# Turning the decayed keys by DMA instead of on TensorE, in a fused linear-attention and feed-forward kernel

## The chip, the cores and the metric

The kernel runs on one core of one Trainium2 chip. The metric is the device time of one execution in microseconds, the median over runs. The core has a matrix engine (TensorE, PE in the profile; its weight loads have a row of their own, PEld), a vector engine (VectorE, DVE), a scalar engine (ScalarE, ACT), GpSimd (POOL), and a queue engine (SyncE, SP) that issues nearly all DMAs here. Each engine works through its own list of instructions in order and waits on semaphores for the others.

## The reference

Two parts, cut to what matters. The first is a linear attention with a decaying state (batch 4, 8 heads, 768 tokens, head size 48):

```python
state = zeros((B, H, D, D))
for t in range(S):
    cur = einsum('bhd,bhe->bhde', u[None] * kt, vt)
    y[:, :, t] = einsum('bhd,bhde->bhe', rt, state + cur)
    state = wt[:, :, :, None] * state + einsum('bhd,bhe->bhde', kt, vt)
```

The second takes the result as 3072 tokens of 384 and is a feed-forward block with 2048 hidden units:

```python
h = x @ w_in
g = h - tanh(h)
out = g @ w_out
```

All inputs and outputs are fp32, and the kernel works in fp32.

## The kernel before

**Blocks.** The 768 tokens of each of 4 sequences are cut in two, which gives eight blocks of 384 tokens (NB). A block has four pairs of heads (one pair fills the 128 partitions: two heads of 48 rows, padded to 64) and six chunks of 64 tokens. Heads are handled in two halves of two pairs each, named by their first pair: half 2 and half 0, in that order (HALVES).

**The attention of a block.** With the transposed keys, receptances and decays loaded with features on partitions, `behind` (L379) makes by a scan the product of the decays from each token to the end of its chunk, and `before` (L372) the same towards the chunk's beginning. `times_behind` (L397) multiplies the keys by the first; the result, the decayed keys, lies in the tile `post`. `earlier` (L462) multiplies decayed keys with decayed receptances within a chunk. `update_1` (L480) needs the decayed keys a second time, with tokens on partitions: `turn` (L465) transposes them on TensorE, twelve squares of 128x128 for a block (two halves, two pairs, three pairs of chunks), into a scratch tile of PSUM for each half, and ScalarE copies each half to the tile `ks` (L473). `update_2` (L500) forms the states, and the result of a block is gathered into `xT` by `result`, `result_out` (ScalarE copies) and `fill_holes` (six small DMAs, L618). `bound` (L414) is a check of the decays on ScalarE: one pass over a half of the tile `w`, with a sum.

**The feed-forward part.** For a block it runs over 16 slices of the hidden units, f = 0 to 15. `first` (L717) makes the hidden values of a slice, hp, by six matmul instructions (L720), and ScalarE copies them out as h (L723). The tile hp has one buffer. `slight` (L729) then squares on ScalarE (L741, L742, L744), and VectorE makes g (L726). In blocks 2 to 7 the second product is done in a form with fewer multiplications (`Fewer`, L821): sums of slices of g on VectorE (L767), products on TensorE (L835), and at a block's end scalings of the banks by ScalarE (`scaled`, L845) in f=1 and f=2 of the next pass. Block 0 and 1 use plain products (L797).

**The order of the work.** The order on TensorE, SyncE, VectorE and ScalarE is the order in which the program emits it. The loop over i (blocks) and f runs the feed-forward part of block i, and weaves in the attention of block i+1 (`later`) and the first scans of block i+2 (`after`). `plan` (L886) says at which f each piece is emitted: `phases` for TensorE's pieces, `before` and `ahead` for the others, `loads` for the DMAs. Within one f the order of emission is: h of this f and its squares; VectorE's waiting pieces; the entries of `before`; the phase; the entries of `ahead`; sums and loads; then second products that have come due and their scalings. In pass i=0 the plan is its own one; passes i=1 to 6 prepare blocks 2 to 7; i=7 prepares nothing. The first block's attention runs ahead of the loop (`boot`, L931) and uses `turn` as well, as does pass i=0 for block 1.

The tiles `w`, `k`, `r`, `post`, `pre` and `ks` have one buffer each, used by one block after the other.

Of the kernel before, what the change touches and what calls it, by code (L numbers as in the profile page):

```python
# [42 lines left out]
U16 = mybir.dt.uint16  # L43
# [8 lines left out]
P = 128  # L52
L = 64
NB = 384
# [6 lines left out]
HALF = WIDE // 2 + 2  # L61
UP = 2
# [58 lines left out]
def kernel(  # L121
# [12 lines left out]
    nc = tc.nc  # L134
# [146 lines left out]
    class Block:  # L281
# [183 lines left out]
        def turn(self, ps, p0, ahead=0):  # L465
# [6 lines left out]
                                        self.chunk("post", p0 + p, 2 * c, n=2), ident)  # L472
            nc.scalar.copy(out=ks.rearrange("t p c d -> t p (c d)"), in_=tp[:, :, 0:NCP * P])  # L473

        def keys(self):
            if not hasattr(self, "ks"):
                self.ks = work.tile([P, NPAIR, NCP, P], F32, name="ks", tag="ks", bufs=1)
            return self.ks
# [142 lines left out]
        def phase(self, ps, name):  # L621

            if name in ("own", "earlier"):
                return [getattr(self, name)(ps, p0) for p0 in HALVES]
            if name == "turn":
                for p0 in HALVES:
                    self.turn(ps, p0)
            elif name == "update":
                self.update_1(ps)
                return [self.update_2]  # L630
            elif name == "result 1":
                self.results(ps)
                self.result("from_states", ALL)
            elif name == "result 2":
                self.result("from_scores", ALL, True)
                self.result_out(ALL)
                self.fill_holes([nc.sync])
            return []
# [247 lines left out]
    def plan(i):  # L886


        converted = ()
        if i == 0:  # L890
            phases = {4: "turn", 6: "update", 8: "own", 11: "earlier", 13: "result 1"}
            before = {0: ("behind 2", "take_whole 2"), 1: ("behind 0", "take_whole 0", "times_behind 2"),
                      2: ("times_behind 0",), 3: ("before 2",), 4: ("times_u 2",), 5: ("before 0", "times_u 0"),
                      8: ("times_before", "held", "bound 2"), 9: ("bound 0",)}
            ahead = {}
            converted = range(READY + 1, NF)
            loads = {f: "weights" for f in (0, 1, 3, 4, 5, 6, 7, 8, 9, 10)}
            loads.update({2: "next r", 11: "w", 12: "k", 13: "r"})
        else:
            phases = {4: "earlier", 7: "turn", 10: "update", 12: "result 1"}  # L900
            before = {0: ("times_behind 2",), 1: ("times_behind 0",), 3: ("times_before", "held"), 4: ("bound 2",),
                      5: ("product_u",), 6: ("bound 0", "product_r"), 7: ("product_sum",), 8: ("diagonal_in 2",),
                      9: ("diagonal_in 0",)}
            if i == 1:
                phases = {6: "earlier", 8: "turn", 10: "update", 12: "result 1"}
                before.update({0: ("behind 2", "take_whole 2"), 1: ("behind 0", "take_whole 0"),
                               2: ("before 2", "times_behind 2"), 3: ("before 0", "times_behind 0"),
                               4: ("times_before", "held", "bound 2")})
            ahead = {10: ("behind 2", "take_whole 2"), 12: ("behind 0", "take_whole 0"), 13: ("before 2",),
                     15: ("before 0",)}  # L910
            loads = {1: "v", 3 + (i == 1): "tokens k", 4 + (i == 1): "tokens r", 7: "w", 9: "k", 11: "r"}
        return phases, before, ahead, converted, loads
# [113 lines left out]
    for i, blk in enumerate(blocks):  # L1026
# [5 lines left out]
        if i == 1:  # L1032
            early.close()
            if fast:
                wide = ctx.enter_context(tc.tile_pool(name="wide", bufs=1))
                forms = wide.tile([P, NF // 2, len(W_FORMS), P], F32, name="forms", tag="forms")
                G = wide.tile([P, 32, P], F32, name="g", tag="g")
        phases, before, ahead, converted, loads = plan(i)
        row0 = blk.b * S + blk.q * NB
        fewer = Fewer(row0, acc, few[i] // 2) if few[i] else None  # L1040
        second = Second(row0, acc, few[i]) if few[i] < NF else None
        for f in range(NF):
# [37 lines left out]
            if not later and f == NF - 2:  # L1080
                at = n_whole + n_excess
# [21 lines left out]
            name, ins = loads.get(f), None  # L1103
# [20 lines left out]
            while due and due[0][0] <= now:  # L1124
                _, add, what = due.pop(0)
# [84 lines left out]
```

## Time and profile before

| What | Value |
|---|---|
| time, three runs | 573.3, 573.57, 575.57 us (median 573.57) |
| span of the profiled execution, first to last instruction | 572.0 us (the page gives no time of its own for this execution) |
| TensorE busy | 553.3 us, 97% |
| VectorE busy | 477.7 us, 84% |
| ScalarE busy | 345.3 us, 60% |
| granted TensorE clock, mean | 0.999 |
| DMA | 50.40 MB, mean 88 GB/s |
| transposes on TensorE (L471) | 96, of which 72 in the passes i=1 to 6 |
| copies of them on ScalarE (L473) | 16, mean 789 ns |

The profile is of one execution. Busy time is a share of the span; durations of matmuls overlap, so the distance from one start to the next is what a matmul costs in a full stretch. A group's idle time is that of its engine just before it, with the releaser behind the arrow. In a timeline a row is: start, length (of the whole group, if several are merged), engine, line, operation, output and input, count, and in brackets the idle time before it. Pass i=4 begins its first products (f=0) at 300.93 us, and the f that follow begin at 306.22, 310.16, 313.44, 316.71, 321.74, 325.02, 328.29, 332.88, 336.15 and 342.11 us (f=1 to 10). The transposes of the passes i=1 to 6 begin at 134.54, 197.58, 264.04, 330.23, 396.41 and 462.72 us.

### The profile page before, as it was taken

How to read it: one execution, taken by the hardware profiler on the slowest of the kernel's cores; microseconds unless marked ns; L12 is line 12 of the kernel's file. 1: busy time of each engine (PE TensorE's matmuls, PEld its weight loads, DVE VectorE, ACT ScalarE, POOL GpSimd, SP SyncE). 2: the span in 40 equal slices, each digit the busy share in tenths (PEclk: the TensorE clock that was granted, in tenths of full speed). 3: DMA queues.
4: the chain of work that ended last, by engine and by line, in shares of the span. 5: the costliest groups of instructions: out<-in, count | busy, mean ns of one | idle time of the engine just before them, and what ended most of it. 6: DMA issues, size and time to landing. Idle time of an engine off the chain costs nothing.

```text
span 572.0 us, 14041 instructions
## 1 busy us (share of the span) xinstructions
PE 553.3 (97%) x5736; PEld 404.7 (71%) x5736; DVE 477.7 (84%) x926; ACT 345.3 (60%) x702; POOL 11.9 (2%) x40
## 2 busy tenths in 40 slices
PE   4889999999999999999999999999999999999996
PEld 4646666566665887777778787777878777787763
DVE  8878884799879989889998989989998998658673
ACT  3979893343137755577566775767556775667441
POOL 6100000000000000000000000000000000000000
PEclk9999999999999999999999999999999999999999
DMA  8496553222203232041212231122221300100101
GB/s 323 174 333 208 180 181 109 83 84 76 92 11 107 69 105 64 5 125 57 74 62 72 84 113 57 53 84 85 72 66 49 120 2 2 44 10 1 41 2 45
DMA packets 32453, 50.40 MB, mean 88 GB/s; under 512 B 2560, under 2 KB 30336, under 8 KB 32384
## 3 DMA queue, kind: packets, MB, share of 16 engines
q1 hardware_dynamic: 32144, 49.38, 26.9%
q8 instruction: 46, 0.75, 0.6%
q14 instruction: 23, 0.19, 0.1%
q0 software_dynamic: 96, 0.07, 0.1%
q10 hardware_dynamic: 144, 0.00, 0.0%
HBM read 43.55 MB, written 4.72 MB: 84 GB/s over the span
## 4 chain that ended last, share of the span: by engine, by line
PE 92%; ACT 2%; DVE 2%; DMA 2%; issue 1%; SPq 0%; DVEq 0%
PE hp L720 42%; PE acc L835 22%; PE acc L797 13%; PE att L835 5%; PE att L447 2%; PE att L471 2%; PE att L561 2%; PE att L496 2%; PE att L578 2%; ACT up L255 1%; DMA r<-in_rT 1%; DMA w<-in_wT 1%; DVE post L387 1%; DVE post L401 0%; ACT w_sb L255 0%
## 5 line engine op out<-in xcount | busy, mean ns | idle before, releaser
L720 PE MATMUL hp<-xT,w_sb 128*128 128x384 f32 x768 | 270.1, 488 | 2.0 <-ACT h L723 1.4
L720 PEld LDWEIGHTS hp<-xT,w_sb 128*128 128x128 f32 x768 | 138.4, 190 | 81.7 <-ACT h L723 4.4
L723 ACT ACTIVATE h<-hp 128x384 f32<-128x384 f32 x128 | 62.6, 489 | 150.2 <-PE hp L720 148.5
L835 PE MATMUL acc<-forms,g 128*128 128x128 f32 x810 | 121.1, 277 | 0.5
L835 PEld LDWEIGHTS acc<-forms,g 128*128 128x128 f32 x810 | 108.7, 192 | 15.6 <-issue 1.2
L767 DVE TENSOR_TENSOR g<-g 128x256 f32<-128x256 f32 x225 | 95.5, 424 | 19.8 <-DVE g L767 0.9
L726 DVE SCALAR_TENSOR_TENSOR h<-h,s 128x384 f32<-128x384 f32 x128 | 70.5, 550 | 10.6 <-ACT s L741 9.9
L797 PE MATMUL acc<-w_sb,sums 128*128 128x384 f32 x192 | 68.1, 491 | 1.6 <-DVE sums L726 1.3
L726 DVE SCALAR_TENSOR_TENSOR g<-qa,h 128x384 f32<-128x384 f32 x96 | 53.6, 558 | 17.1 <-PE acc L835 4.0
L742 ACT ACTIVATE qa<-s,shift 128x384 f32<-128x384 f32 x90 | 55.4, 615 | 2.9
L744 ACT ACTIVATE junk<-s,shift 128x384 bf16<-128x384 f32 x90 | 53.9, 599 | 0.0
L797 PEld LDWEIGHTS acc<-w_sb,sums 128*128 128x128 f32 x192 | 35.6, 190 | 25.9 <-DVE sums L726 2.6
L741 ACT ACTIVATE s<-h 128x384 f32<-128x384 f32 x90 | 47.1, 523 | 2.9
L835 PE MATMUL acc<-w_sb,g 128*128 128x128 f32 x270 | 44.9, 275 | 0.0
L752 ACT ACTIVATE qa<-s,shift 128x384 f32<-128x384 f32 x38 | 23.2, 611 | 24.7 <-DVE top L749 24.7
L835 PEld LDWEIGHTS acc<-w_sb,g 128*128 128x128 f32 x270 | 37.4, 192 | 0.0
L749 DVE CUSTOM_DVE_ANT_0 s<-h 128x384 f32<-128x384 f32 x38 | 21.0, 553 | 12.8 <-ACT h L723 12.8
L255 ACT ACTIVATE up<-raw 128x768 f16<-128x768 f32 (+1 forms) x32 | 31.7, 1056 | 0.0
L726 DVE SCALAR_TENSOR_TENSOR sums<-qa,h 128x384 f32<-128x384 f32 x32 | 17.9, 558 | 15.6 <-ACT qa L752 12.2
L835 PE MATMUL att<-w_sb,g 128*128 128x128 f32 x180 | 30.2, 275 | 0.0
L835 PEld LDWEIGHTS att<-w_sb,g 128*128 128x128 f32 x180 | 26.4, 192 | 4.5
L387 DVE TENSOR_TENSOR_SCAN post<-w,seed 128x780 f32<-128x780 f32 x16 | 28.5, 1784 | 1.1 <-DMA w<-in_wT 1.0
(87 smaller groups left out, 529.1 us busy)
## 6 DMA issues: line engine op xcount, KB each, us to landing
raw<-in_weights SPq DMA_DIRECT2D x16, 768.0 KB, 4.4
w<-in_wT SPq DMA_DIRECT2D x7, 780.0 KB, 4.6
k<-in_kT SPq DMA_DIRECT2D x7, 768.0 KB, 4.7
r<-in_rT SPq DMA_DIRECT2D x7, 768.0 KB, 4.5
v_sb<-in_v SPq DMA_DIRECT2D x8, 576.0 KB, 4.2
k<-in_tokens SPq DMA_DIRECT2D x6, 576.0 KB, 3.9
r<-in_tokens SPq DMA_DIRECT2D x6, 576.0 KB, 4.0
out_y<-sums SPq DMA_DIRECT2D x15, 128.0 KB, 1.9
```

The costliest lines, as they stand in the source:

```text
L255: return lambda: nc.scalar.activation(out=to, in_=of, func=AF.Copy, scale=scale, bias=bias)
L387: return nc.vector.tensor_tensor_scan(out=back(t[:, 0:width]), data0=back(self.tile("w")[:, a:a + width]), data1=back(seed[:, 0:width]), i ...
L720: nc.tensor.matmul(hp, lhsT=w_in_sb[:, f, kc, :], rhs=xT[kc], start=(kc == KC - 1), stop=(kc == 0))
L723: return h, nc.scalar.activation(out=h, in_=hp, func=AF.Copy, scale=1.0 / UPSCALE)
L726: return lambda: nc.vector.scalar_tensor_tensor(out=out, in0=in0, scalar=scalar, in1=in1, op0=op0, op1=ALU.mult)
L741: nc.scalar.activation(out=s, in_=h, func=AF.Square)
L742: nc.scalar.activation(out=qa, in_=s, func=AF.Square, bias=shift[:, 4:5])
L744: nc.scalar.activation(out=junk[:, 0:NB], in_=s, func=AF.Relu, bias=shift[:, 5:6], accum_out=excess[:, at:at + 1])
L752: first = [lambda: nc.scalar.activation(out=qa, in_=s, func=AF.Square, bias=shift[:, 4:5])]
L767: return lambda: nc.vector.tensor_tensor(out=G[:, to:to + 2], in0=two(G, g_at(q, a0), g_at(q, a1)), in1=two(G, g_at(q, b0), g_at(q, b1)), ...
L797: nc.tensor.matmul(acc, lhsT=g[:, j * P:(j + 1) * P], rhs=w_out_sb[:, f, :], start=(f == self.first), stop=(f == NF - 1))
L835: nc.tensor.matmul(to, lhsT=G[:, g_at(q, a), :], rhs=rhs, start=start, stop=stop, skip_group_check=True)
```

## The change

For the six blocks that are prepared in passes i=1 to 6 the phase "turn" is taken out of the plan. In its place stand four phases, two for each half:

- `split` copies a half of the decayed keys on ScalarE, read as 16-bit words, into two planes (all low halves of the 32-bit values, then all high halves). Then SyncE issues one DMA that transposes the planes in squares of 128x128 16-bit elements. Half 2 uses the second half of the tile `w` for its planes and the place of half 0 in `ks` for the result; half 0 uses the place of half 2 in `post` for the planes and its own place in `post` for the result.
- `join` copies the transposed planes on ScalarE back into 32-bit values in `ks`, as 16-bit words.

A half is 128 partitions of 768 fp32 values, 1536 words of 16 bits. In passes i=2 to 6 the phases stand at f=2 (split 2), f=5 (join 2), f=6 (split 0) and f=9 (join 0), and bound 2 moves from f=4 to f=1. In pass i=1 they stand at f=4, 7, 8 and 10, bound 2 moves from f=4 to f=3, the update from f=10 to 11 and the result from f=12 to 13. Blocks 0 and 1 keep the transposes on TensorE.

```diff
+        def words(self, t, at=0):
+            return t[:, at:at + UP * NB].bitcast(U16)
+
+        def split(self, p0):
+            self.turned = (self.keys()[:, 0:UP].rearrange("t p c d -> t (p c d)").bitcast(U16) if p0
+                           else self.words(self.tile("post")))
+            words = self.words(self.tile("w" if p0 else "post"), HALF + 2)
+            nc.scalar.copy(out=words.rearrange("d (two t) -> d two t", two=2),
+                           in_=self.tokens("post", p0, UP).bitcast(U16).rearrange("d (t two) -> d two t", two=2))
+            nc.sync.dma_start_transpose(out=self.turned.rearrange("t (n d) -> t n d", d=P), in_=words)
+
+        def join(self, p0):
+            dst = self.keys()[:, p0:p0 + UP].rearrange("t p c d -> t (p c d)").bitcast(U16)
+            nc.scalar.copy(out=dst.rearrange("t (n two) -> t two n", two=2),
+                           in_=self.turned.rearrange("t (two n) -> t two n", two=2))
+
...
             if name == "turn":
                 for p0 in HALVES:
                     self.turn(ps, p0)
+            elif name.startswith(("split", "join")):
+                what, p0 = name.split()
+                getattr(self, what)(int(p0))
...
-            phases = {4: "earlier", 7: "turn", 10: "update", 12: "result 1"}
-            before = {0: ("times_behind 2",), 1: ("times_behind 0",), 3: ("times_before", "held"), 4: ("bound 2",),
+            phases = {2: "split 2", 4: "earlier", 5: "join 2", 6: "split 0", 9: "join 0", 10: "update", 12: "result 1"}
+            before = {0: ("times_behind 2",), 1: ("times_behind 0", "bound 2"), 3: ("times_before", "held"),
                       5: ("product_u",), 6: ("bound 0", "product_r"), 7: ("product_sum",), 8: ("diagonal_in 2",),
                       9: ("diagonal_in 0",)}
             if i == 1:
-                phases = {6: "earlier", 8: "turn", 10: "update", 12: "result 1"}
+                phases = {4: "split 2", 6: "earlier", 7: "join 2", 8: "split 0", 10: "join 0", 11: "update", 13: "result 1"}
                 before.update({0: ("behind 2", "take_whole 2"), 1: ("behind 0", "take_whole 0"),
-                               2: ("before 2", "times_behind 2"), 3: ("before 0", "times_behind 0"),
-                               4: ("times_before", "held", "bound 2")})
+                               2: ("before 2", "times_behind 2"), 3: ("before 0", "times_behind 0", "bound 2"),
+                               4: ("times_before", "held")})
```

## The prediction

> **What bounds the kernel now.** I read the page's busy shares first, then the busy time by stretches for one block, then the groups of instructions by shape, the waits, and last the timelines of TensorE and ScalarE through the stage that the change edits.
>
> ```profile
> PE 553.3 (97%) x5736; PEld 404.7 (71%) x5736; DVE 477.7 (84%) x926; ACT 345.3 (60%) x702; POOL 11.9 (2%) x40
> 302.90:369.10 66.20, 66.09 (x718) 52.03 (x717) 59.49 (x116) 42.59 (x94) 0.14 (x2) 1.00 0.25 74
> ```
>
> The second line is one period of the loop, a pass of sixteen f (columns: window, length, then busy PE, PEld, DVE, ACT, POOL, clock, DMA share, GB/s). TensorE is busy for 66.09 of 66.20 us, so what leaves it shortens the kernel, and what makes it wait lengthens it. ScalarE has 23.6 us free on average, but an average does not tell where. The transposes and their copies, by shape:
>
> ```profile
> L471 PE MATMUL att<-ident,post 128*128 128x128 f32 x96 | 13.4, 292 | 5.4 <-DVE post L401 5.4
> L473 ACT COPY ks<-att 128x768 f32<-128x768 f32 x16 | 11.9, 789 | 1.1 <-PE att L471 1.1
> PE hp L720 <- ACT h L723: 1.4, 3, 0.6
> ```
>
> The last line is from the waits: TensorE's first product (L720) waits for ScalarE's copy of the one before (L723), since hp has one buffer. Today that is 1.4 us in all. TensorE in the loop pass i=4 (f=6 and f=7; start, length of the group):
>
> ```profile
> 325.02 2.10 PE L720 MATMUL hp<-xT,w_sb 128*128 128x384 f32 x6
> ...
> 328.29 2.10 PE L720 MATMUL hp<-xT,w_sb 128*128 128x384 f32 x6
> 330.23 1.47 PE L471 MATMUL att<-ident,post 128*128 128x128 f32 x12
> ...
> 332.88 2.10 PE L720 MATMUL hp<-xT,w_sb 128*128 128x384 f32 x6
> ```
>
> An ordinary f takes 328.29 - 325.02 = 3.27 us, the one with twelve transposes 4.59. ScalarE in the same pass, at f=2 to 3 and at f=5 to 7:
>
> ```profile
> 314.40 0.19 ACT L744 ACTIVATION_READ_ACCUMULATOR junk<-s,shift 128x1 f32 x1
> 314.50 1.06 ACT L846 ACTIVATE sums<-acc 128x512 f32<-128x512 f32 x2
> 315.57 0.49 ACT L723 ACTIVATE h<-hp 128x384 f32<-128x384 f32 x1
> ...
> 325.99 0.19 ACT L744 ACTIVATION_READ_ACCUMULATOR junk<-s,shift 128x1 f32 x1
> 327.15 0.49 ACT L723 ACTIVATE h<-hp 128x384 f32<-128x384 f32 x1 [0.98 <-PE hp L720]
> ...
> 329.48 0.94 ACT L418 ACTIVATE junk<-w,shift 128x780 bf16<-128x780 f32 x1
> 330.33 0.19 ACT L418 ACTIVATION_READ_ACCUMULATOR junk<-w,shift 128x1 f32 x1
> 330.43 0.49 ACT L723 ACTIVATE h<-hp 128x384 f32<-128x384 f32 x1
> ```
>
> At f=2 (two scalings, L846) and at f=6 (the bound, L418) no idle time stands before the next h copy: ScalarE is exactly full there. An ordinary f leaves 0.98 us.
>
> **What is removed.** The twelve transposes cost 4.59 - 3.27 = 1.32 us of TensorE's time, and in six blocks 7.9 us. All of it is on the path. The two copies L473 at f=7 go too (1.48 us for both), but 0.91 us of idle stood behind them, so that alone gives nothing.
>
> **How much lateness TensorE forgives.** The h copy of f=5 starts 2.14 us after its products and ends at 324.37; the next products start at 325.02. Minus 0.05 for the hand-over (h ends at 180.63, hp starts at 180.68 in the one place where it waits now), an h copy may be 0.60 us late for nothing; beyond that every microsecond stalls TensorE.
>
> **What a split and a join cost.** Each handles 1536 16-bit elements, which no row shows. Start to start (ScalarE overlaps the tail of one with the next), 384 elements take 0.38 us (L611, x3 in 1.25) and 768 take 0.69 (L473, x2 in 1.48), so 768 further elements are 0.62. The weight conversion has the strided forms: 768 with a strided source 0.80, with a strided 16-bit destination too 0.92 (x2 in 1.97). A split has a strided source: 0.80 + 0.62 = 1.42 if the stride costs once, 1.60 if per element; I take 1.50. A join has a strided 16-bit destination: 1.54 to 1.84; I take 1.70. The ends for both are 1.31 (dense) and 1.84. The Trainium skill, "ScalarE: Activation LUTs", section "What ACT_TABLE_LOAD costs", says that an ACTIVATE with immediate operands takes 186 ns plus 0.833 ns an element in fp32 and bf16 alike, less 93 ns back to back; that would be 1.37 us for each and, by the sum below, 574.9 us; this trace does not agree for strided 16-bit writes, 0.92 for 768 where the rule gives 0.73.
>
> **Where they fall in i=2 to 6.** Split 2 comes behind the h copy of f=2 and its squares, ahead of the scalings: h of f=3, on time today at 315.57, is 1.50 late, and TensorE stalls 1.50 - 0.60 = 0.90 at hp of f=4 (partly sooner, since the sums of f=3 wait for bank 1 to be scaled). The lateness left, 0.60, goes in the idle of f=3. Join 2 at f=5 has 1.06 us from the read at 325.99 (next start 326.09) to 327.15: 1.70 makes h of f=6 0.64 late. Split 0 at f=6 stands behind the bound, where nothing is free: h of f=7 is 0.64 + 1.50 = 2.14 late, and TensorE stalls 1.54 in all there. At f=7 the missing copies let ScalarE catch up. Join 0 at f=9 has 2.79 us idle ahead of the next h (as at 283.08 and 344.25): nothing, unless the update needs it sooner. Sum: 0.90 + 1.54 = 2.44 lost, 1.32 won, 1.12 worse a block.
>
> **The other moves.** Bound 2 goes from f=4 to f=1, where 1.17 us idle before h at 312.30 covers its 1.05; in i=2 only 0.44 is free there, but f=2 has 0.49 more, and the sum of that block stays about the same. In i=1 ScalarE idles over 2 us in an f, so the split and the joins cost nothing, and the 1.32 is won whole. Update and result one f later there: the last hole's transfer lands at about 159.24 + 3.73 + 1.9 = 164.9 against first products at 170.26; 3.87 later still leaves 1.5 us. The pass is one f closer to its end, and a cover below 3.87 would be paid in full.
>
> **The transposes.** Twelve squares, 384 KB a half. Rows on both sides: the xT holes, 24 KB in 1.9 us, and twelve such one after another, 22.8 us. The nearest rows move the same bytes:
>
> ```profile
> k<-in_kT SPq DMA_DIRECT2D x2, 384.0 KB, 5.3
> r<-in_rT SPq DMA_DIRECT2D x2, 384.0 KB, 6.2
> ```
>
> I take 6.2. From the end of split 2 (316.0) to join 2's place (326.09 + 0.90) there are 11.0 us; from the end of split 0 (330.43 + 0.90 + 0.64 + 1.50 = 333.47) to the last moment at which join 0 doesn't hold up the update (344.14 + 1.12 - 1.70 = 343.56) there are 10.1; in i=1, where split 0 and join 0 stand two f apart, about 9.5. So they are hidden, and queued on SP ahead of tokens k (issued at 316.09, landing near 320, used on VectorE at 324.15) and of w (330.95, used some 14 us later), which can be late by 4 and 9 us. POOL's memsets of post (L382), which wait for the transposes now, will wait for the joins; they are read only in the next pass. VectorE waits for a transpose only in i=1, where the next block's scan writes over its source from 6.8 us on.
>
> **The sum.** 5 x 1.12 - 1.32 = +4.3 us. The page gives the profiled execution's span, 572.0, and no time of its own; the runs' median of 573.57 stands 1.6 above, start and end that the change leaves alone. 573.57 + 4.3 = 577.9. With both copies at 1.31 it is 574.0, at 1.84 582.0 (the loss is two splits plus a join minus 2.26).
>
> **Rivals.** *Cheap copies (faster).* The place is f=2 and f=6: if 16-bit elements went at two for one of 32 bits, a split and a join cost 0.69 like L473, h is 0.09 late at most twice, the loss is 0.18 a block, and it is 573.57 + 5 x 0.18 - 7.9 = 566.6. Even is reached at 1.28 us a copy, 0.5% faster at 1.09. Against it: L418 with bf16 output takes 0.94 for 780 elements and L744 0.60 for 384, 0.86 ns an element, nothing saved. For it: TensorE's 97%, and that neither instruction is in the trace. 0.19.
>
> *Late transposes (much slower).* A join waits for its transfer on ScalarE, in order, and with it the h copies: from 11.0 us on each microsecond is lost at join 2, from 10.1 at join 0. At 11.5 us it is 5 x (0.5 + 1.4) more, 587 to 588; at 22.8 over 120 more, 700. For it: a row of a square is 256 bytes, and of 32453 packets here only 2560 are under 512; against it: 5.3 to 6.2 for the same bytes. 0.17. The Trainium skill, "VectorE: DVE Perf Modes", section "The three transpose paths", gives 1309 ns for a 128x128 bf16 transpose by DMA against 390 on TensorE; twelve in a row would be an estimated 15.7 us and about 630, and no row here shows whether they overlap.
>
> *Nothing to be seen.* The lateness is made up elsewhere just as far as the transposes gave: 573 to 575. 0.05.
>
> **How the numbers follow.** The forecast, late h copies with hidden transposes, has 0.59: most of it above +0.5% (576.4), some 0.16 below, for copies near the dense price. With 0.5% as about what a measurement of this kernel can tell from no change: slower 0.43 + 0.17 = 0.60, same 0.16 + 0.05, faster 0.19. The range takes in the cheap copies, from 566, and the dear ones with a transpose at 11.5 us, 588; what lies above, most of the late transposes, is left out. The forecast's own range is 574 to 582.
>
> **What would show it.** Right: no L471 in the six blocks, ACT copies 128x1536 of 1.4 to 1.9 us, waits "PE hp <- ACT h" grown from 1.4 to about 12 us, at f=4 and f=8, and h copies there with no idle ahead of them. Wrong: copies below 1.1 us; or ScalarE's joins waiting for a DMA; or stalls of TensorE that name VectorE, which has 59.5 of 66.2 us busy and is also fed later.

## The result, and the profile after

The changed kernel takes 578.57 us (median of 4 runs, 577.35 to 578.91) beside 574.16 for the kernel before; the ratio is 1.0073 [1.0052, 1.0095], so it is 0.7% slower, 4.2 us [3.0, 5.5]. In a second set of runs it was 1.0069 [1.0054, 1.0084]. The forecast was 577.9 from 573.57, a ratio of 1.0075.

The page of after, the line of busy times, and three lines of the groups by shape and of the waits (engine, line, what it waited for: us in all, times, longest):

```profile
PE 549.6 (95%) x5664; PEld 398.5 (69%) x5664; DVE 478.2 (83%) x926; ACT 373.1 (65%) x714; POOL 11.8 (2%) x40
```

```profile
L490 ACT COPY ks<-post 128x1536 uint16<-128x1536 uint16 x6 | 11.5, 1916 | 0.0
L484 ACT COPY w<-post 128x1536 uint16<-128x1536 uint16 x6 | 8.8, 1459 | 0.0
```

```profile
PE hp L741 <- ACT h L744: 7.7, 11, 1.1
```

TensorE has 72 instructions less, is less busy, and the kernel is longer. ScalarE has 28 us more to do. The wait of the first product for ScalarE's h copy went from 1.4 to 7.7 us on TensorE's own row. (Line numbers moved: L720 is now L741, L723 is L744, L835 is L856.)

The timeline of TensorE in pass i=4, at f=3 to 4 and f=6 to 8:

```profile
318.05 0.49 PE L856 MATMUL acc<-w_sb,g 128*128 128x128 f32 x2
318.37 0.39 PE L856 MATMUL acc<-forms,g 128*128 128x128 f32 x2
318.92 2.20 PE L741 MATMUL hp<-xT,w_sb 128*128 128x384 f32 x6 [0.15 <-ACT h L744]
...
327.32 2.10 PE L741 MATMUL hp<-xT,w_sb 128*128 128x384 f32 x6
...
330.69 2.20 PE L741 MATMUL hp<-xT,w_sb 128*128 128x384 f32 x6
...
335.31 2.20 PE L741 MATMUL hp<-xT,w_sb 128*128 128x384 f32 x6 [1.08 <-ACT h L744]
```

From f=7 to f=8 TensorE takes 335.31 - 330.69 = 4.62 us. With the twelve transposes in it, it took 4.59. Where the transposes stood there is now a wait about as long: 4.62 - 3.27 = 1.35 us by the starts, of which the row names 1.08. ScalarE in the same stretches:

```profile
316.05 1.46 ACT L484 COPY w<-post 128x1536 uint16<-128x1536 uint16 x1
317.42 1.07 ACT L867 ACTIVATE sums<-acc 128x512 f32<-128x512 f32 x2
318.38 0.48 ACT L744 ACTIVATE h<-hp 128x384 f32<-128x384 f32 x1
...
328.39 1.91 ACT L490 COPY ks<-ks 128x1536 uint16<-128x1536 uint16 x1
330.16 0.48 ACT L744 ACTIVATE h<-hp 128x384 f32<-128x384 f32 x1
...
332.47 0.94 ACT L418 ACTIVATE junk<-w,shift 128x780 bf16<-128x780 f32 x1
333.32 0.19 ACT L418 ACTIVATION_READ_ACCUMULATOR junk<-w,shift 128x1 f32 x1
333.42 1.46 ACT L484 COPY post<-post 128x1536 uint16<-128x1536 uint16 x1
334.78 0.48 ACT L744 ACTIVATE h<-hp 128x384 f32<-128x384 f32 x1
```

No idle time stands before any of these three h copies. Split to the next start is 317.42 - 316.05 = 1.37 us, a join 1.77.

A finer measure than the time is the length of a pass, from the first h copy of one pass to that of the next (before, i=4: 303.07 to 369.25). It leaves out what stands ahead of the loop and pass i=0, which are the same code in all kernels and still differed from one profiled execution to another (first h copy at 29.6 to 36.5 us). Differences to before, in us; the third column is the ratio of times with its interval. Where the text below says how far a kernel is from before, it goes by this ratio; before was measured again beside each set of runs, with medians of 573.56, 573.65 and 574.08 us.

| Kernel | i=1, 2, 3, 4, 5, 6: sum | ratio to before |
|---|---|---|
| the change | -1.31, 0.73, 0.97, 0.98, 0.85, 0.98: +3.2 | 1.0073 [1.0052, 1.0095] |
| the change, again | -1.31, 0.73, 1.07, 1.26, 0.85, 0.97: +3.6 | 1.0069 [1.0054, 1.0084] |
| no DMA transposes | -1.31, 0.73, 1.08, 0.97, 0.92, 0.97: +3.4 | 1.0070 [1.0048, 1.0093] |
| bound 0 at f=4 | -1.31, -0.34, 0.50, 0.73, 0.62, -0.09: +0.1 | 1.0018 [0.9997, 1.0039] |
| half copies | -1.31, -0.82, -0.20, -0.04, -0.33, -0.98: -3.7 | 0.9947 [0.9928, 0.9965] |
| nothing turned | -1.31, -1.08, -0.45, -0.18, -0.53, -1.31: -4.9 | 0.9921 [0.9907, 0.9936] |
| room on ScalarE | -1.31, -0.78, -0.37, -0.44, -0.26, -1.31: -4.5 | 0.9944 [0.9929, 0.9958] |
| room, states sooner | -1.31, -0.77, -1.32, -1.22, -0.58, -0.51: -5.7 | 0.9918 [0.9899, 0.9937] |
| that, diagonal later | -1.30, -0.62, -1.32, -0.34, -0.65, -1.01: -5.2 | 0.9926 [0.9903, 0.9949] |

### The profile page after: what moved, and what is told of

The parts are those of the page before. It is cut to its first block, busy times and chain, and to the rows that moved or that the text cites. A ratio compares the mean times of both kernels' runs of the same rounds, so it can differ in the third digit from the quotient of the medians.

```text
span 576.7 us, 13934 instructions
## 1 busy us (share of the span) xinstructions
PE 549.6 (95%) x5664; PEld 398.5 (69%) x5664; DVE 478.2 (83%) x926; ACT 373.1 (65%) x714; POOL 11.8 (2%) x40
## 4 chain that ended last, share of the span: by engine, by line
PE 79%; ACT 12%; issue 3%; DMA 2%; DVE 2%; SPq 0%; POOL 0%; ACTq 0%; DVEq 0%
PE hp L741 37%; PE acc L856 16%; PE acc L818 12%; PE att L856 5%; PE att L447 2%; ACT h L744 2%; PE att L579 2%; PE att L514 2%; PE att L596 2%; ACT junk L765 2%; ACT ks L490 2%; DMA w<-in_wT 1%; ACT s L762 1%; ACT post L484 1%; ACT w L484 1%
## 5 line engine op out<-in xcount | busy, mean ns | idle before, releaser
L741 PE MATMUL hp<-xT,w_sb 128*128 128x384 f32 x768 | 271.6, 490 | 10.5 <-ACT h L744 7.7
L741 PEld LDWEIGHTS hp<-xT,w_sb 128*128 128x128 f32 x768 | 138.3, 190 | 92.7 <-ACT h L744 12.9
L744 ACT ACTIVATE h<-hp 128x384 f32<-128x384 f32 x128 | 62.5, 488 | 123.8 <-PE hp L741 119.9
L856 PE MATMUL acc<-forms,g 128*128 128x128 f32 x810 | 121.0, 277 | 0.6
L856 PEld LDWEIGHTS acc<-forms,g 128*128 128x128 f32 x810 | 109.1, 192 | 16.9 <-issue 1.2
L856 PE MATMUL acc<-w_sb,g 128*128 128x128 f32 x270 | 45.3, 277 | 0.3
L856 PEld LDWEIGHTS acc<-w_sb,g 128*128 128x128 f32 x270 | 37.4, 192 | 1.0 <-ACT sums L867 1.0
L856 PE MATMUL att<-w_sb,g 128*128 128x128 f32 x180 | 30.2, 275 | 0.0
L856 PEld LDWEIGHTS att<-w_sb,g 128*128 128x128 f32 x180 | 26.4, 192 | 4.5
```

The costliest lines, as they stand in the source:

```text
L741: nc.tensor.matmul(hp, lhsT=w_in_sb[:, f, kc, :], rhs=xT[kc], start=(kc == KC - 1), stop=(kc == 0))
L744: return h, nc.scalar.activation(out=h, in_=hp, func=AF.Copy, scale=1.0 / UPSCALE)
L856: nc.tensor.matmul(to, lhsT=G[:, g_at(q, a), :], rhs=rhs, start=start, stop=stop, skip_group_check=True)
```

## The experiments

My theory was that ScalarE delivers h late at two places in a pass because of the copies. The rivals: the DMA transposes cost the time, by being late or by their traffic; or the copies don't matter and VectorE sets the pace.

**The change again**, as the reference for the runs beside it:

> The changed kernel once more, as the reference point for the runs beside it. Theory (late h copies on ScalarE): the starts of the h copies put the passes i=2 to 6 at +0.7 to +1.0 us each against before and pass i=1 at -1.3, so +3.2 us in all, about 577 beside 573.6 to 574.2 for the kernel before; what the first comparison showed above that (4.4 us) stands ahead of the loop, where the code is the same, and need not come back. Rival (the transposes' DMA traffic slows other work in general): more than 3.2 us, spread over all f.

577.24 us, passes as before. The transposes' traffic is no part of it as far as this goes: outside f=1 to 3, 5 to 8 and 12 no step from one h copy to the next changed by more than 0.05 us in the passes 2 to 6.

**No DMA transposes.** The splits and joins stay, the DMA goes:

```diff
-            nc.sync.dma_start_transpose(out=self.turned.rearrange("t (n d) -> t n d", d=P), in_=words)
+            self.turned = words
```

> The change with all its splits and joins but without the DMA transposes: a join reads the planes of its split, so the keys of blocks 2 to 7 stay unturned. Theory (late h copies): the h copies start as in the change, passes i=2 to 6 at +0.7 to +1.0 us against before, i=1 at -1.3, and the time is the change's, 577, within 1 us. Rival (the transposes in flight, their SP time or their traffic, cost the time): it falls to or below the time of the kernel before, 573.6.

577.78 us, ratio 1.0070, passes +3.4. Taking the transposes away leaves the loss as it is, so it is in the copies and their places. The rival that the transposes cost the time is out.

**Half of the copies.** Only the plane of the high halves is split and joined:

```diff
-            nc.scalar.copy(out=words.rearrange("d (two t) -> d two t", two=2),
-                           in_=... .rearrange("d (t two) -> d two t", two=2))
+            nc.scalar.copy(out=words.rearrange("d (two t) -> d two t", two=2)[:, 1],
+                           in_=... .rearrange("d (t two) -> d two t", two=2)[:, 1])
```

and the same `[:, 1]` in `join`. In this kernel and in the next one, with nothing turned, `ks` is one fixed tile.

> The change with splits and joins over the plane of the high halves alone, 768 elements instead of 1536; the low halves of the keys are not turned (ks keeps stale ones). The DMAs are as in the change. Theory (late h copies by the length of the copies): a split of about 0.75 and a join of about 0.95 us leave at most 0.15 us of stall at f=2 and at f=6; the transposes' 1.32 us a block is won until VectorE's states bind in passes 3 to 5: 4 to 5 us faster than before, 569. Rival (the DMAs or the number of instructions cost the time): as slow as the change, 577.

570.87 us, ratio 0.9947 [0.9928, 0.9965]: 3.0 us faster than before, where 4 to 5 were expected. The groups by shape:

```profile
L492 ACT COPY ks<-post 128x768 uint16<-128x768 uint16 x6 | 6.3, 1047 | 0.0
L486 ACT COPY w<-post 128x768 uint16<-128x768 uint16 x6 | 4.9, 819 | 0.0
```

With shorter copies and the same DMAs the sign turns. The stalls at f=2 to 8 fell from 2.3 to 0.3 us a pass. What else is lost lies at f=12 in passes 3 to 5, 0.65 to 0.94 us, as in the next experiment, and at f=1 in pass 2, 0.5 us for bound 2.

**Nothing turned.** Splits, transposes and joins all gone:

```diff
-            phases = {2: "split 2", 4: "earlier", 5: "join 2", 6: "split 0", 9: "join 0", 10: "update", 12: "result 1"}
+            phases = {4: "earlier", 10: "update", 12: "result 1"}
...
-                phases = {4: "split 2", 6: "earlier", 7: "join 2", 8: "split 0", 10: "join 0", 11: "update", 13: "result 1"}
+                phases = {6: "earlier", 11: "update", 13: "result 1"}
```

> The change without splits, transposes and joins: the keys of blocks 2 to 7 are not turned, and their updates use what block 1 left in ks; bound 2 at f=1 and the later update and result of pass i=1 stay. It measures what the twelve transposes a block were worth. Theory: 6 x 1.32 = 7.9 us faster than before, about 566, with no h copy late. If it gains clearly less, another engine (VectorE) takes over as bound, and the loss of the change is not all in the copies.

569.08 us, ratio 0.9921 [0.9907, 0.9936]: 4.5 us faster, not 7.9. Each of the six passes does win 1.31 us at the place of the transposes, but passes 3 to 5 lose 0.8 to 1.1 us again at f=12. Bound 2 costs pass 2 another 0.5 us at f=1. The timeline of this kernel at f=12 of pass i=4, TensorE and then VectorE:

```profile
353.64 0.33 PE L583 MATMUL att<-pre,states 48*64 48x64 f32 x4
354.42 1.62 PE L583 MATMUL att<-pre,states 48*64 48x64 f32 x92 [0.45 <-DVE states L540]
```

```profile
353.92 0.35 DVE L540 TENSOR_TENSOR states<-states,att 128x192 f32<-128x192 f32 x1
354.31 0.36 DVE L530 TENSOR_TENSOR states<-states,whole 128x192 f32<-128x192 f32 x1
```

TensorE waits for states that VectorE is still making: VectorE ends L540 at 354.27, and TensorE goes on at 354.42. In the kernel before, in the same pass (L540 is L518 there, L583 is L561):

```profile
351.88 0.35 DVE L518 TENSOR_TENSOR states<-states,att 128x192 f32<-128x192 f32 x1
```

```profile
352.43 1.63 PE L561 MATMUL att<-pre,states 48*64 48x64 f32 x96
```

VectorE ended the same work at 352.23 and TensorE came 0.20 us later: just in time, so no wait showed. VectorE's work ahead of that point has not become shorter, and in passes 3 to 5 most of what TensorE saves is lost at f=12. The wait shown is 0.45 of the 1.14 us that this pass loses there. When VectorE makes the states sooner, in an experiment below, f=12 of this pass loses nothing.

**Bound 0 away from split 0.**

```diff
-                      5: ("product_u",), 6: ("bound 0", "product_r"), ...
+                      5: ("product_u",), 4: ("bound 0",), 6: ("product_r",), ...
```

> The change with bound 0 moved from f=6, where it stands ahead of split 0 on ScalarE, to f=4, where ScalarE has over 2 us idle; pass i=1 keeps it at f=6. Theory (late h copies): split 0 then stands alone at f=6; h of f=7 is late by 0.71 + 1.37 - 1.06 = 1.02 us instead of 2.1, the stall at f=5 to 8 falls from 1.54 to 0.42, and each of the passes i=2 to 6 is 1.1 us shorter than in the change: 5.5 us faster than the change, some 2 us faster than the kernel before. Rival (transposes in flight cost the time): nothing moves, since the DMAs stay; within 0.5 us of the change.

573.67 us: 3.6 us below the change and level with before, 1.0018 [0.9997, 1.0039]. At f=5 to 8 the stall fell from 1.54 to 0.47 us in every pass, 0.42 expected. But 0.6 to 0.8 us came back at f=12 in passes 3 to 5, which the expectation didn't have. One edit on ScalarE without touching a DMA moves the time by as much as the whole loss.

**Room on ScalarE.** All six pieces where ScalarE has idle time:

```diff
-            phases = {2: "split 2", 4: "earlier", 5: "join 2", 6: "split 0", 9: "join 0", ...
-            before = {0: ("times_behind 2",), 1: ("times_behind 0", "bound 2"), 3: ("times_before", "held"),
-                      5: ("product_u",), 6: ("bound 0", "product_r"), ...
+            phases = {1: "split 2", 4: "earlier join 2", 5: "split 0", 9: "join 0", ...
+            before = {0: ("times_behind 2", "bound 2"), 1: ("times_behind 0",), 3: ("times_before", "held", "bound 0"),
+                      5: ("product_u",), 6: ("product_r",), ...
```

> The same copies and DMAs, put where ScalarE has idle time: bound 2 at f=0, split 2 at f=1, bound 0 at f=3, join 2 at f=4, split 0 at f=5, join 0 at f=9 (passes i=2 to 6; pass i=1 only moves bound 0 back to f=6 as in the change). Theory (late h copies): no h copy is over 0.6 us late, except in i=2 at f=1, 0.3; the 1.32 us of each of six blocks is won: 7.6 us faster than before, about 566.3. Rival (DMA traffic, or longer transfers met by the shorter gaps, 9 us from split 2 to join 2): still slower than before. Rival (VectorE becomes the bound, 59.5 of 66.2 us busy): less than half of the 7.6.

569.75 us, ratio 0.9944 [0.9929, 0.9958], 3.2 us below before; 7.6 were expected. ScalarE no longer holds anything up at f=2 to 8 (0.0 us of stall); pass 2 loses 0.8 at f=1, where 0.3 was expected. For the rest the passes are as those with nothing turned, with 0.9 to 1.1 us lost at f=12 in passes 3 to 5. By the time this is less than half of the 7.6, as the second rival, VectorE, had it; by the passes it is 4.5. Either way the 2.9 us of f=12, VectorE's, are the largest part of what is missing.

**The states sooner.** The next block's scan behind 2 goes behind the states:

```diff
-            ahead = {10: ("behind 2", "take_whole 2"), 12: ...
+            ahead = {10 + (i > 1): ("behind 2", "take_whole 2"), 12: ...
```

> The placement of the kernel with splits and joins where ScalarE has room, and the next block's scan behind 2 at f=11 instead of f=10 in passes i=2 to 6, so that VectorE makes the states (update_2) 1.95 us sooner. Theory: the 0.9 to 1.1 us that h of f=13 lost in passes 3 to 5 there are TensorE waiting for the last states at f=12, because VectorE's work up to the states has not become shorter while TensorE's has; with the states sooner that goes, and about 3 us more are won: 566 to 567, 7 us below before. Rival (VectorE is simply full: the wait comes back elsewhere, at f=14 to 16 or in the next pass): no more than 1 us better than the placement alone, 569.

568.68 us, ratio 0.9918 [0.9899, 0.9937], 4.7 us below before; 7 were expected. f=12 is clean in passes 3 and 4, which now win their whole 1.2 to 1.3 us, but passes 5 and 6 lose 0.4 to 0.6 us there and 0.2 to 0.3 at f=4. So the outcome lies between theory and rival: with VectorE's order changed the wait at f=12 is gone in passes 3 and 4 and about halved in 5, but it is new in pass 6, and f=4 is new in both. The same move in the kernel before:

> The kernel before, transposes on TensorE, with only behind 2 moved from f=10 to f=11 in passes i=2 to 6. Theory: in the kernel before TensorE reaches the states just as VectorE has them, it waits 0.3 us in one pass, so the move alone is worth under 0.5 us: 573.2 to 573.6. Rival (the move itself is the gain): 2 us or more faster than before.

573.38 us, 0.9997 [0.9979, 1.0016]: nothing, as expected. The move shows a gain only once TensorE has been relieved.

**The diagonal later.** On top of that:

```diff
-                      9: ("diagonal_in 0",)}
+                      9 + 2 * (i > 1): ("diagonal_in 0",)}
```

> The kernel with room on ScalarE and the states sooner, with one more piece of VectorE's work, diagonal_in 0 (1.0 us), moved from f=9 to f=11, behind the states, in passes i=2 to 6. Theory (VectorE's order ahead of the states binds): the 0.4 to 0.6 us that passes 5 and 6 still lost at f=12 go; about 1 us better than that kernel, 567.5 to 568.5. Rival (VectorE is full over the whole pass): no better than 568.7, or worse, with TensorE waiting for the scores of half 0 at the end of f=12.

569.68 us, 0.9926 [0.9903, 0.9949]: no better. The wait at f=12 went, and 0.5 to 0.8 us came up at f=15 in passes 4 and 5, with a name that had 0.3 us in the list of the kernel with the states sooner:

```profile
PEld acc L859 <- DVE g L791: 2.0, 3, 1.0
```

The second products wait for VectorE's sums. The rival was right here: VectorE is busy for 59.9 of the 65.8 us of pass 4, and its order only moves the wait.

**Four transposes for one.**

```diff
-            nc.sync.dma_start_transpose(out=..., in_=words)
+            for _ in range(4):
+                nc.sync.dma_start_transpose(out=..., in_=words)
```

> The change with each transpose issued four times, the same planes to the same place. Theory (transposes are hidden, with 11.0 us from split 2 to join 2 and 10.1 for the second half): what counts is when the last one lands. One lands 3.7 us after its issue, of which 1.3 to 1.4 us are SP's. If they go one after the other, 15 us: 4 us lost at join 2 and 5 at join 0 in five passes, 40 to 50 us more than the change, 620. If they overlap behind the issue, 4 x 1.35 + 2.4 = 7.8 us: no change, 577. Rival (the traffic of the transposes is what costs 3 to 4 us): three times that more, 587 to 590, with no join waiting.

651.56 us, 1.137 [1.1339, 1.1401]: 74 us above the change where 40 to 50 were expected for transposes one after another. SP's timeline, SP's waits, and the waits of the engines:

```profile
358.00 14.14 SPq L487 DMA_TRANSPOSE ks<-w  x4
372.25 0.82 SPq L339 DMA_DIRECT2D k<-in_tokens  x1
```

```profile
SPq L487 <- DMA ks<-w: 47.7, 18, 3.8
SPq L487 <- DMA post<-post: 38.0, 18, 3.7
```

```profile
DVE k L343 <- DMA k<-in_tokens: 62.3, 6, 12.8
...
ACT ks L491 <- DMA ks<-w: 28.0, 5, 7.8
ACT ks L491 <- DMA post<-post: 25.9, 6, 7.8
...
PE att L515 <- ACT ks L491: 16.9, 6, 5.8
...
PE acc L819 <- DVE sums L748: 10.6, 2, 9.4
```

Transposes that land late do hold up the joins, 54 us in all, as the prediction's rival "late transposes" had it. (The waits overlap, so they don't add.) They go one after another because SP issues each only when the one before has landed: its waits name the earlier transfer to the same place. So this run doesn't show how several in flight would fare, and four times the traffic without a wait stays untested. The passes 2 to 6 are 54 us longer than in the change, 9 to 13 each, where 9 were expected. Most of what made it dearer is pass 1, 19 us, which the expectation left out: there VectorE waits 12.8 us for the tokens of k, which stand behind the transposes in SP's queue, TensorE waits 9.4 us for VectorE's sums, and 5.8 us more for the second join.

## Why the prediction was right

*Transposes on TensorE, 1.32 us a block, all on the path:* 1.31 us in pass 1, where nothing stands against it, and 1.31 in each pass with nothing turned.

*The copies:* split 1.50 taken, 1.37 measured start to start; join 1.70, 1.77 measured. At f=2 the h copy came 1.25 us late instead of 1.50: the split's 1.37, less about 0.1 that the two scalings still had to give (0.96 to the next start instead of 1.07), so ScalarE was not quite full there. At f=5 to 7 it was 0.70 and 1.34, 2.04 together instead of 2.14. The 0.60 that TensorE forgives held, but the prediction lacked one term: the products behind a stall take 2.20 us instead of 2.10. So the stalls are 1.25 - 0.60 + 0.10 = 0.75 us at f=2 to 4 and 2.04 - 0.60 + 0.10 = 1.54 at f=5 to 8, where 0.90 and 1.54 were forecast. That the second comes out to the hundredth is luck: two misses of 0.10 cancel. The split was priced too high: it takes 1459 ns for 1536 elements and 819 for 768, 0.83 ns an element. The Trainium skill, "ScalarE: Activation LUTs", section "What ACT_TABLE_LOAD costs", gives 186 ns plus 0.833 ns an element, an estimated 1.466 us for 1536; the split agrees. The join, with its 16-bit writes two apart, takes 1.91 and does not.

*The sum:* +1.12 a pass was forecast, +0.73 to +0.98 came; with -1.31 for pass 1, +3.2 instead of +4.3. The time grew by 4.2 us [3.0, 5.5], so that 1.0 us lies outside the passes 1 to 6 (0.4 in the second set). The ratio of 1.0073 beside the 1.0075 forecast is thus in part luck. In the profiled execution 1.2 us of the difference lies ahead of pass 1, where the first products wait 2.45 us for a small transfer, and 0.3 behind the last h copy; the code is the same there, and in the run without DMA transposes the start of pass 1 came 0.1 us sooner than before. Why all kernels of the table stand 0.4 to 1.3 us above their passes, also with nothing turned, stays open; an interval reaches 0.8 to 1.3 us to either side.

*The transposes hidden:* 3.7 and 3.3 us from issue to landing, 6.2 taken, against 11.0 and 10.1 of room:

```profile
ks<-w SPq DMA_TRANSPOSE x6, 3.7
post<-post SPq DMA_TRANSPOSE x6, 3.3
```

The Trainium skill, "VectorE: DVE Perf Modes", section "The three transpose paths", gives 1309 ns for one 128x128 square, which for twelve in a row would have been an estimated 15.7 us. Twelve in one transfer take 3.2 to 5.3 here, so that sum does not hold; no run times a single square. The tokens behind them on SP land later (median 5.4 us for r, 4.0 before). In passes 2 to 6 nobody waits for them; in pass 1 VectorE waits 1.4 us for those of k, which the prediction did not have, and the 0.44 us by which the h copy of f=8 comes late with it is made up in that f. Without the DMA transposes neither is there.

*Bound 2, the later update and result of pass 1:* 0.51 us in pass 2, where the prediction's 1.05 less 0.44 gives 0.61, and it is made up at f=2, as forecast. Pass 2 does not wait for the holes.

*What would show it:* h copies without idle ahead of them, and waits at f=4 and f=8: as forecast. The size was off on TensorE's row, 7.7 us instead of 12, because part of the stall at f=3 is a wait for the bank that ScalarE scales later (L856 at 318.05), as the prediction had said in passing. The list has it only on the row of the weight loads (PEld):

```profile
PEld acc L856 <- ACT sums L867: 1.0, 4, 0.3
```

*What the prediction lacked:* VectorE's part. It was named as what would make the forecast wrong, by its busy share alone. In the change itself it costs almost nothing (up to 0.3 us at f=12), probably since ScalarE's stalls give VectorE time; no run tests that. But it means that the cheap-copies rival, priced at 566.6, would hardly have come out in this plan: with nothing turned at all it is 569.1.

## What to carry to other kernels

Before work is moved from a full engine to one that is 60% busy, look for the stretch in which it is to be put: two places with no idle ahead of a copy on the path cost more than all that was saved, and the same work elsewhere in the pass made it a gain of 0.6%, or 0.8% with one of VectorE's scans moved too. An engine that arrives just in time shows no wait; before counting a saving whole, look at how late each input of the relieved engine becomes ready, not only at what it waits for today. A queue that has to wait for one transfer before it issues the next holds back what stands behind it: the four transposes kept SP for 14 us, and VectorE waited for tokens that only stood behind them.

## What the runs showed of the hardware that I had not expected

A DMA transpose of 128 x 1536 16-bit elements, twelve squares, occupies SP for 1.3 to 1.6 us at its issue, against 0.37 to 0.47 for a plain load of k of up to 768 KB, and lands 3.2 to 5.3 us after. ScalarE reads 16-bit elements two apart at 0.83 ns each (1.46 us for 1536, 0.82 for 768) but writes them so at 1.13 (1.91 and 1.05); no run copies such elements with both sides dense. The six products behind a wait for h took 2.20 us instead of 2.10, all of it in the first (590 ns instead of 488).
